# GLU first blocks packed into one PSUM bank, spectral filter rows used at their own pitch, last output in three pieces

## The chip, the cores and the metric

The kernel runs on one core of one Trainium2 chip. Its engines work side by side, each through its own queue in order: TensorE (PE in the profile, its weight loads PEld) for matmuls, VectorE (DVE), ScalarE (ACT), GpSimd (POOL), and SyncE (SP), which here only issues DMAs. The metric is device time in microseconds (us), lower is better. The time before is the median of three runs. The profile is of one more execution, with a time of its own.

## What is computed

The input is 2048 rows of 512 in bf16. A layer norm over each row feeds two branches, whose sum with the input is the output:

```python
xn = _layernorm(x, axis=-1)                       # x: (1, 2048, 512)

# branch A: filter in the frequency domain
X = rfft2(xn, axes=(-2, -1)) * (w_r + 1j * w_i)   # w_r, w_i: (2048, 257)
a = irfft2(X, s=(2048, 512)).astype(bfloat16)

# branch B: gated linear unit
g = xn @ w_gate ; u = xn @ w_up                   # (512, 1792) each
b = (gelu(g) * u) @ w_down                        # (1792, 512)

out = x + a + b
```

## The kernel before

**Tiling.** Row 16p+c of the input is held in partition p, column c: `x_t` and `xn` are [128, 16, 512], and "column c" below means 128 input rows. The 1792 hidden features are 14 weight slices of 128 (`fc`). Four columns form a super-block `sb`, so there are four. For the GLU the normalised rows are needed transposed (`xnT[sb]`): columns 0 to 3 are transposed on TensorE and copied out of PSUM by ScalarE (`pe_transpose`, L445 to L455), columns 4 to 15 by DMA transposes issued by SyncE (L458).

**Order.** Nothing is written in program order. Every piece of work is an operation with an engine, an assumed duration, dependencies, a priority (smaller goes first) and the rings of buffers it takes or frees. `_Plan.run` (L149) plays the list on a model of the engines and emits each operation when the model starts it; on the chip each engine then takes its instructions strictly in that order and waits by semaphores. Loads are modelled in one line of bytes at 0.3e6 bytes per us plus 0.8 us (L195, L196), at most eight in flight. The assumed durations and rates thus decide the order, and nothing else.

**PSUM.** Eight banks: four of tag S (transposes, spectral stages, and the down projection), two of tag G for the gate product, two of tag U for the up product.

**GLU.** `glu(c0, n, fc)` (L492) takes n columns from c0 and one weight slice: four matmuls over 512 inputs into a G bank, four into a U bank (L506), gelu on ScalarE into `ge` (L515), and the product on VectorE into `hT` (L520). The first super-block is done in small units while data arrives: columns 0 and 1 alone with slices 0 and 1, columns 0 and 1 together with slices 2 and 3, columns 2 and 3 with slices 0 to 3, then four columns at a time (L529 to L532). A unit of n columns issues matmuls of 128n wide. Each uses 128n of a bank's 512 columns.

**Start.** x columns 0 to 3 come as four loads, weights in groups 0-1, 2-3, then x 4 to 7, weights 4-6, x 8 to 11, weights 7-9 and 10-13, x 12 to 15 (L334 to L348). `layernorm` takes statistics (L427), adds epsilon (L435), raises to -1/2 on GpSimd (L437) and normalises (L440). TensorE runs ten dummy matmuls from the start, and four small ones after each of the columns 0 and 1 (L406 to L418, `NGAP`).

**Spectral branch.** `fold` (VectorE, L548 to L560, then `bp` matmuls L574), `dstep` (L610, evicted at L615), `cstep` (L630, L638) take the forward transform; `filt` (L644) multiplies by the filter for one of eight groups g; `icstep` (L748) and `idstep` (L796, L802 and the combining at L818 to L824) go back. In `filt`, steps `s3` (L671) and `s4` (L677) multiply 1024 elements by the real and the imaginary filter rows; for g = 0, `s10` (L705 to L708) redoes one partition with seven short instructions as one operation.

**Filter table.** `TW` is [128, 2, 8, 2, 258]: real and imaginary, group, two rows per group, 257 values padded to 258. The weights have 257 values a row, so seven groups of rows are first loaded unpadded into `Ts` (by SyncE at L363, and by indirect DMAs of GpSimd at L365 for the mirrored rows) and then spread by twelve ScalarE copies into `TW` (`spread`, L376, with reversed group order for the mirrored rows); the rows of group 0 come by four more indirect DMAs (L397). GpSimd then mends a few columns (`tables_fix`, L588), which `s3` waits for. `Ts` shares its memory with `Wd`, the down weights, so these are loaded after the copies (L391).

**End.** `down(c)` (L832) sums 14 matmuls with the down weights (L848) and one with the last stage of the inverse transform (L852) in a PSUM bank, adds x on VectorE (L857) and stores (L860). The last column is done in two halves of 256.

Of the kernel before, what the change touches and what calls it, by code (L numbers as in the profile page):

```python
# [10 lines left out]
P = 128  # L11
# [6 lines left out]
S = 2048  # L18
# [110 lines left out]
class _Plan:  # L129
# [19 lines left out]
    def run(self):  # L149
# [11 lines left out]
        while left:  # L161
            nxt, moved = None, False
            for e, ops in waiting.items():
# [30 lines left out]
                if o.nbytes:  # L194
                    wire = max(wire, o.end + 1.0) + o.nbytes / 0.3e6  # L195
                    o.end = wire + 0.8  # L196
                    lanes.append(o.end)
                    lanes = [x for x in lanes if x > now]
# [19 lines left out]
def kernel(  # L218
# [18 lines left out]

    x_v = A_x.rearrange("b (p c) d -> p c (b d)", c=NC)
# [4 lines left out]
    KC = 257  # L243
# [13 lines left out]
    TW = pc.tile([P, 2, NG, 2, 258], BF16, name="TW", tag="TW")  # L257
    TR, TI = TW[:, 0], TW[:, 1]
# [81 lines left out]
    load_x(2, 1)  # L340
    load_x(3, 1)
    load_w(2, 4)
    load_x(4, 4)
    load_w(4, 7)
    load_x(8, 4)
    load_w(7, 10)
# [7 lines left out]
    R7 = 7 * KC  # L354
    d_st = {}

    def load_rows(k, s, h):
        if "Ts" not in tiles:
            tiles["Ts"] = pc.tile([P, 2, 2, R7], BF16, name="Ts", tag="Wd")
        w_in = (A_w_r, A_w_i)[k]  # L360
        rows = w_in.rearrange("(kb t h a g) k -> t h kb a (g k)", kb=NC, t=2, h=2, a=4)
        if s == 0:
            nc.sync.dma_start(out=tiles["Ts"][64 * h:64 * h + 64, k, s], in_=rows[0, h][:, :, KC:8 * KC])  # L363
        else:
            nc.gpsimd.indirect_dma_start(  # L365
                out=tiles["Ts"][:, k, s], out_offset=None, in_=w_in[:, :],
                in_offset=bass.IndirectOffsetOnAxis(ap=idx_t[:, 2:3], axis=0))

    for k in range(2):
        for s in range(2):  # L370
            if s == 0:
                d_st[k, s] = [load(64 * R7 * 2, lambda k=k, s=s, h=h: load_rows(k, s, h)) for h in range(2)]
            else:
                d_st[k, s] = [add("POOL", 1.2, lambda k=k, s=s: load_rows(k, s, 0), (g_idx, XD[12]), 20, lag=5.0)]

    def spread(k, s, g0, g1):  # L376
        T = (TR, TI)[k]
        src = tiles["Ts"][:, k, s].rearrange("p (g k) -> p g k", k=KC)
        src = src[:, g0 - 1:g1 - 1] if s == 0 else src[:, 7 - g1 + 1:7 - g0 + 1][:, ::-1]
        nc.scalar.copy(out=T[:, g0:g1, s, 0:KC], in_=src)  # L380

    for k in range(2):
        for s in range(2):
            for g0, g1 in ((1, 3), (3, 5), (5, 8)):
                d_tw.append(act(0.2 + (g1 - g0) * 0.215, lambda k=k, s=s, g0=g0, g1=g1: spread(k, s, g0, g1),
                                d_st[k, s], 40 + len(d_tw)))

    def load_wd(k):
        if "Wd" not in tiles:
            tiles["Wd"] = pc.tile([P, NFC, D], BF16, name="Wd_sb", tag="Wd")  # L390
        nc.sync.dma_start(out=tiles["Wd"][:, 7 * k:7 * k + 7], in_=wd_v[:, 7 * k:7 * k + 7])  # L391

    d_wd = [load(P * 7 * D * 2, lambda k=k: load_wd(k), d_tw[:12]) for k in range(2)]

    for T, w_in in ((TR, A_w_r), (TI, A_w_i)):
        for s in range(2):
            d_tw.append(add("POOL", 1.2, lambda T=T, w_in=w_in, s=s: nc.gpsimd.indirect_dma_start(  # L397
                out=T[:, 0, s, 0:KC], out_offset=None, in_=w_in[:, :],
                in_offset=bass.IndirectOffsetOnAxis(ap=idx_t[:, s:s + 1], axis=0)), (g_idx, XD[12]), 20, lag=4.0))
# [6 lines left out]
    NWARM, NGAP, GAP = 10, 2, 4  # L406
# [22 lines left out]
    def layernorm(c0, n, due, after=()):  # L429
# [9 lines left out]
        for c in range(c0, c0 + n):  # L439
            XN[c] = dve(0.36, lambda c=c: V.tensor_scalar(  # L440
                out=xn[:, c], in0=x_t[:, c], scalar1=mv[:, c, 0:1], scalar2=rstd[:, c:c + 1],
                op0=ALU.subtract, op1=ALU.mult), (r,), due - 2.5)
        return ag

    def pe_transpose(c, due):  # L445
        b = _Buf("S")

        def mm():
            tp = psum(f"tp.{c}", [P, NE, P], BF16)
            for e in range(NE):  # L450
                nc.tensor.transpose(tp[:, e], xn[:, c, e * P:(e + 1) * P], ident)

        o = pe(0.24, mm, (XN[c], d_ident), due - 2, new=(b,))
        XT[c] = act(0.45, lambda: nc.scalar.copy(out=xnT[c // 4][:, :, c % 4], in_=tiles[f"tp.{c}"][:]),  # L454
                    (o,), due - 30, use=(b,))  # L455

    def dma_transpose(c, due):
        XT[c] = dma(P * D * 2, lambda: nc.sync.dma_start_transpose(out=xnT[c // 4][:, :, c % 4], in_=xn[:, c]),  # L458
                    (XN[c],), due - 30, lag=1.0)

    first = ()
    for c, due in ((0, -28), (1, -25), (2, -22), (3, -19)):
        o = layernorm(c, 1, due, first if c == 1 else ())
        first = o if c == 0 else first
        pe_transpose(c, due)
        if c < NGAP:
            dummies(GAP, due - 1.9, (XN[c],), P)
# [10 lines left out]
    def hslot(sb, fc):  # L478
        if (sb, fc) not in tiles:
            if sb < 3:  # L480
                t = pc.tile([P, NFC, 512], BF16, name=f"hT{sb}", tag=("hT0", "hT1", "xn")[sb])
                tiles.update({(sb, f): t[:, f] for f in range(NFC)})
            else:
                m = min(4, NFC - fc)
                t = pc.tile([P, m, 512], BF16, name=f"hT3{fc}", tag=("xnT0", "xnT1", "xnT2", "hT3")[fc // 4])
                tiles.update({(sb, fc + f): t[:, f] for f in range(m)})
# [3 lines left out]
    done_g = {b: [] for b in range(NSB)}  # L490

    def glu(c0, n, fc, extra=()):  # L492
        sb, o, w = c0 // 4, (c0 % 4) * P, n * P
        gb, ub, eb = _Buf("G"), _Buf("U"), _Buf("ge")
        key = f"{c0}.{n}.{fc}"
        t = now[0]
        dur = 4 * (w / 2400.0 + 0.0024)
        now[0] += 2 * dur + 0.2
# [4 lines left out]
        def mm(nm, W, tag):  # L503
            p = psum(f"{nm}.{key}", [P, D], tag=tag)
            for e in range(NE):
                nc.tensor.matmul(p[:, 0:w], lhsT=W[:, e, fc * P:(fc + 1) * P], rhs=rhs(e),  # L506
                                 start=(e == 0), stop=(e == NE - 1))

        xt = [XT[c] for c in range(c0, c0 + n)]
        g = pe(dur, lambda: mm("g_ps", Wg_sb, "G"), xt + [WD[fc][0]], t, new=(gb,))  # L510
        u = pe(dur, lambda: mm("u_ps", Wu_sb, "U"), xt + [WD[fc][1], g], t, new=(ub,))

        def ge():
            e = work(f"ge.{key}", [P, D], "ge")
            nc.scalar.activation(out=e[:, 0:w], in_=tiles[f"g_ps.{key}"][:, 0:w], func=AF.Gelu_apprx_tanh)  # L515

        a = act(0.1 + w / 1200.0, ge, (g,), t - 40, new=(eb,), use=(gb,))

        def mul():
            V.tensor_tensor(out=hslot(sb, fc)[:, o:o + w], in0=tiles[f"u_ps.{key}"][:, 0:w],  # L520
                            in1=tiles[f"ge.{key}"][:, 0:w], op=ALU.mult)

        h = dve(0.08 + w / 960.0, mul, [u, a] + list(extra), t - 40, use=(ub, eb))
        done_g[sb] += [g, u]
# [378 lines left out]
```

## Time and profile before

| | |
|---|---|
| Time, three runs | 181.13 us median (180.74 to 181.51) |
| Profiled execution | 181.31 us, of which 179.5 from the first to the last instruction |
| TensorE: granted clock | 1.000 |
| DMA | 19.24 MB, mean 107 GB/s, 359 to 409 GB/s in the busiest slices before 23 us |
| GLU matmuls of 512 columns (L506) | 416 of 496; the rest are 256 or 128 wide |
| gelu (L515) at 512, 256, 128 columns | 607, 386, 277 ns |
| product into `hT` (L520) at 512, 256, 128 columns | 686, 410, 285 ns |
| eviction of a transposed column (L454) | 587 ns, 4 times |
| spreading copies (L380) | 12, 738 ns mean, from 29.0 to 46.7 us |
| First `idstep` matmul (L796) | 117.6 us |

The engine shares are averages over stages. Until about 28 us loads run at full rate; from 57 to 108 us the filter groups and the GLU share VectorE; after 122 us TensorE does the down projection with the other engines mostly idle. In a timeline each line gives start, length, engine, line, operation, output <- inputs, and in brackets how long the engine was idle before and what released it. A matmul's listed length contains a modelled pipeline tail, so consecutive rows overlap.

### The profile page before, as it was taken

The numbers are of one execution on the slowest core, as the hardware profiler recorded it, in microseconds if no ns is written. First come the engines' busy times: TensorE is split into PE (matmuls) and PEld (weight loads), VectorE is DVE, ScalarE is ACT, GpSimd is POOL, SyncE is SP. The second block draws the span as 40 slices with busy tenths as digits, with TensorE's granted clock in tenths as the row PEclk, the third lists the DMA queues.
The fourth block names the chain that finished last, engine by engine and source line by source line (L and its number), as shares of the span: only waits on it lengthen the run. The fifth ranks groups of instructions, "written<-read, shape, count | busy, mean of one in ns | idle before, by whom it ended". The sixth has DMA issues, their size and how long they took to land.

```text
span 179.5 us, 2986 instructions
## 1 busy us (share of the span) xinstructions
PE 173.6 (97%) x1057; PEld 91.0 (51%) x1057; DVE 117.9 (66%) x269; ACT 95.6 (53%) x176; POOL 16.4 (9%) x31
## 2 busy tenths in 40 slices
PE   7899999899999999999999999999999999999993
PEld 2596445355554553555555545545445444544462
DVE  1889995999534999989989793436541641632521
ACT  3354225999989849999997945453111211211100
POOL 3404265033200000000000000000000000000000
PEclk9999999999999999999999999999999999999999
DMA  5999999952494002311222022000122231222211
GB/s 146 328 359 347 409 283 160 180 87 58 79 358 151 0 0 55 68 29 29 60 58 64 13 45 45 17 0 0 60 87 64 78 97 58 88 82 68 79 47 50
DMA packets 23182, 19.24 MB, mean 107 GB/s; under 512 B 8256, under 2 KB 21952, under 8 KB 23168
## 3 DMA queue, kind: packets, MB, share of 16 engines
q1 hardware_dynamic: 22176, 17.57, 36.5%
q0 software_dynamic: 320, 1.19, 2.0%
q10 hardware_dynamic: 672, 0.30, 0.6%
q8 instruction: 8, 0.13, 0.3%
q14 instruction: 6, 0.05, 0.1%
HBM read 13.28 MB, written 2.10 MB: 86 GB/s over the span
## 4 chain that ended last, share of the span: by engine, by line
PE 73%; DMA 9%; DVE 7%; SPq 6%; issue 2%; ACT 1%; ACTq 0%; DVEq 0%
PE u_ps L506 18%; PE g_ps L506 17%; DMA Ts<-in_A_w_r_dram 7%; SPq L325 3%; DMA Wu_sb<-in_B_w_up_dram 2%; PE yp L796 2%; PE gp L748 2%; SPq L315 2%; DVE hT L520 2%; PE yp__2064 L848 2%; PE yp__2037 L848 2%; PE yp__2006 L848 2%; PE yp__1921 L848 2%; PE yp__1890 L848 2%; PE yp__1863 L848 2%; PE yp__1832 L848 2%
## 5 line engine op out<-in xcount | busy, mean ns | idle before, releaser
L506 PE MATMUL u_ps<-xnT,Wu_sb 128*128 128x512 bf16 (+2 forms) x248 | 58.2, 358 | 0.6 <-DVE hT L520 0.6
L506 PE MATMUL g_ps<-xnT,Wg_sb 128*128 128x512 bf16 (+2 forms) x248 | 58.2, 358 | 0.5 <-ACT xnT L454 0.5
L520 DVE TENSOR_TENSOR hT<-u_ps,ge 128x512 bf16<-128x512 f32 (+2 forms) x62 | 39.0, 634 | 21.7 <-PE u_ps L506 17.9
L515 ACT ACTIVATE ge<-g_ps 128x512 bf16<-128x512 f32 (+2 forms) x62 | 35.0, 564 | 21.9 <-PE g_ps L506 15.6
L506 PEld LDWEIGHTS <-Wu_sb 128*128 128x128 bf16 x248 | 23.5, 98 | 24.3 <-issue 1.2
L506 PEld LDWEIGHTS <-Wg_sb 128*128 128x128 bf16 x248 | 23.2, 98 | 22.0 <-issue 0.8
L848 PEld LDWEIGHTS <-hT 128*128 128x128 bf16 x238 | 22.7, 98 | 22.0
L802 ACT CAST yf<-yp 128x512 bf16<-128x512 f32 x16 | 9.3, 586 | 38.1 <-PE yp L796 38.1
L638 ACT CAST E<-ep 64x512 bf16<-64x512 f32 x32 | 18.5, 579 | 1.0 <-PE ep L630 0.5
L427 DVE BATCH_NORM_STATS2 st<-x_t 128x6 f32<-128x512 bf16 x16 | 10.7, 675 | 4.3 <-DMA x_t<-in_A_x_dram 4.3
L380 ACT COPY TW<-Ts 128x514 bf16<-128x514 bf16 (+1 forms) x12 | 8.3, 738 | 3.2 <-DMA Ts<-in_A_w_r_dram 3.2
L615 ACT CAST ds<-dp 128x512 bf16<-128x512 f32 x16 | 9.0, 590 | 1.1 <-PE dp L610 1.0
L754 ACT CAST Gs<-gp 128x512 bf16<-128x512 f32 x16 | 8.7, 592 | 1.5 <-PE gp L748 1.5
L437 POOL TENSOR_TENSOR rstd<-ve,half 128x1 f32<-128x1 f32 (+1 forms) x7 | 6.7, 955 | 24.8 <-DVE ve L435 24.8
L578 ACT CAST Bs<-bp 128x512 bf16<-128x512 f32 x16 | 8.7, 633 | 0.0
L411 PE MATMUL warm<-warm 128*128 128x512 bf16 (+1 forms) x18 | 5.5, 469 | 1.3 <-POOL half L404 1.3
L440 DVE TENSOR_SCALAR xn<-x_t,mv,rstd 128x512 bf16<-128x512 bf16 x16 | 6.2, 421 | 0.7 <-POOL rstd L437 0.7
L796 PEld LDWEIGHTS <-Gs 128*128 128x128 bf16 x64 | 4.8, 98 | 3.5
L796 PE MATMUL yp<-CT,Gs 128*128 128x128 bf16 x64 | 6.0, 219 | 0.0
L671 DVE TENSOR_TENSOR m<-X,TW 128x1024 bf16<-128x1024 bf16 x8 | 5.5, 688 | 0.1
L630 PE MATMUL ep<-ds,CT 128*128 128x512 bf16 x16 | 5.6, 379 | 0.0
L677 DVE TENSOR_TENSOR m<-X,TW 128x1024 bf16<-128x1024 bf16 x8 | 5.5, 684 | 0.0
(106 smaller groups left out, 171.1 us busy)
## 6 DMA issues: line engine op xcount, KB each, us to landing
y<-in_A_x_dram SPq DMA_DIRECT2D x16, 128.0 KB, 2.1
F<-F SPq DMA_DIRECT2D x32, 64.0 KB, 2.0
out_dram<-y SPq DMA_DIRECT2D x15, 128.0 KB, 1.7
Wd_sb<-in_B_w_down_dram SPq DMA_DIRECT2D x2, 896.0 KB, 6.3
x_t<-in_A_x_dram SPq DMA_DIRECT2D x3, 512.0 KB, 8.3
Wg_sb<-in_B_w_gate_dram SPq DMA_DIRECT2D x2, 384.0 KB, 7.4
Wu_sb<-in_B_w_up_dram SPq DMA_DIRECT2D x2, 384.0 KB, 8.2
x_t<-in_A_x_dram SPq DMA_DIRECT2D x4, 128.0 KB, 3.4
```

The costliest lines, as they stand in the source:

```text
L380: nc.scalar.copy(out=T[:, g0:g1, s, 0:KC], in_=src)
L427: V.bn_stats(out=st[:], in_=x_t[:, c])
L506: nc.tensor.matmul(p[:, 0:w], lhsT=W[:, e, fc * P:(fc + 1) * P], rhs=rhs(e), start=(e == 0), stop=(e == NE - 1))
L515: nc.scalar.activation(out=e[:, 0:w], in_=tiles[f"g_ps.{key}"][:, 0:w], func=AF.Gelu_apprx_tanh)
L520: V.tensor_tensor(out=hslot(sb, fc)[:, o:o + w], in0=tiles[f"u_ps.{key}"][:, 0:w], in1=tiles[f"ge.{key}"][:, 0:w], op=ALU.mult)
L578: nc.scalar.copy(out=o, in_=tiles[f"bp.{cg}.{q}"][:].rearrange("p c (r g a) -> p (c r) g a", r=2, a=4))
L615: nc.scalar.copy(out=ds[:].rearrange("p (s k t) -> p s k t", s=2, t=2), in_=tiles[f"dp.{G}"][:].rearrange("p s t k -> p s k t"))
L638: nc.scalar.copy(out=tiles[f"E.{g}"][64 * h:64 * h + 64, r], in_=tiles[f"ep.{g}.{h}"][64 * r:64 * r + 64])
L754: nc.scalar.copy(out=o, in_=tiles[f"gp.{g}.{h}"][:].rearrange("p q (n a) -> p (q n) a", a=4))
L796: nc.tensor.matmul(yp[:, q], lhsT=tiles["G"][:, q, c], rhs=IQ[q], start=(q == 0), stop=(q == 3), skip_group_check=True)
L802: nc.scalar.copy(out=tiles[f"yf.{c // 2}"][:, c % 2], in_=tiles[f"yp.{c}"][:])
L848: nc.tensor.matmul(y[:, s], lhsT=tiles[sb, f][:, cl * P:(cl + 1) * P], rhs=tiles["Wd"][:, f, s], start=(f == 0), stop=False)
```

## The change

Five groups of edits.

1. **First blocks.** `glu(c0, n, f0, nf)` now takes nf weight slices for n columns into one bank, each at its own 128n columns of it, with one gelu and one product over nf x 128n columns. The gate and up matmuls are issued two slices at a time. The first super-block becomes six packed units and then slices 6 to 13 for four columns. Loads are regrouped: x columns 2 and 3 in one, weights in 0-1, 2-3, 4-5 ahead of x 4 to 7, then 6-9 and 10-13. The planner's load model becomes 0.34e6 bytes per us plus 1.0 us.
2. **Start.** Column 0 is normalised, transposed and evicted in two halves, the second eviction by VectorE. Columns 2 and 3 share one `layernorm`, whose statistics wait for column 0's evictions. One set of small dummies instead of two.
3. **Filter table.** `TW` becomes [128, 2, 2, 8 x 257] without padding; the loads and indirect DMAs write it directly, `Ts` and the copies are gone, and `s3`, `s4`, `s10` and `tables_fix` read and write it at pitch 257, the mirrored rows in descending group order. The down weights have their own tile and load after the last forward fold.
4. **Filter order.** `s10` is planned as seven operations; buffers `ds` and `E` are claimed by the matmul ahead of the eviction, and the four `E` evictions are no longer chained to the first.
5. **End.** The down projection uses the G and U banks in turn, and the last column is done in pieces of 256, 128 and 128.

The core of the diff:

```diff
-                    wire = max(wire, o.end + 1.0) + o.nbytes / 0.3e6
-                    o.end = wire + 0.8
+                    wire = max(wire, o.end + 1.0) + o.nbytes / 0.34e6
+                    o.end = wire + 1.0
...
-    TW = pc.tile([P, 2, NG, 2, 258], BF16, name="TW", tag="TW")
-    TR, TI = TW[:, 0], TW[:, 1]
+    TW = pc.tile([P, 2, 2, NG * KC], BF16, name="TW", tag="TW")
...
-    load_x(2, 1)
-    load_x(3, 1)
+    load_x(2, 2)
     load_w(2, 4)
+    load_w(4, 6)
     load_x(4, 4)
-    load_w(4, 7)
+    load_w(6, 10)
     load_x(8, 4)
-    load_w(7, 10)
     load_w(10, 14)
...
+    def rows_at(s, g):
+        return (7 - g if s else g) * KC
+
+    def pair(k, g, p=P):
+        a = TW[0:p, k, 0, rows_at(0, g):rows_at(0, g) + 256]
+        step = NG * KC + rows_at(1, g) - rows_at(0, g)
+        return bass.AP(a.tensor, a.offset, [a.ap[0], [step, 2], [1, 256]])
+
+    def load_rows(k, h):
+        rows = (A_w_r, A_w_i)[k].rearrange("(kb t h a g) k -> t h kb a (g k)", kb=NC, t=2, h=2, a=4)
+        nc.sync.dma_start(out=TW[64 * h:64 * h + 64, k, 0, KC:], in_=rows[0, h][:, :, KC:8 * KC])
+
+    def gather(k, s, c, a, n):
+        w_in = (A_w_r, A_w_i)[k]
+        nc.gpsimd.indirect_dma_start(
+            out=TW[:, k, s, a:a + n], out_offset=None, in_=w_in[:, :],
+            in_offset=bass.IndirectOffsetOnAxis(ap=idx_t[:, c:c + 1], axis=0))
...
-    def spread(k, s, g0, g1):
-        T = (TR, TI)[k]
-        src = tiles["Ts"][:, k, s].rearrange("p (g k) -> p g k", k=KC)
-        src = src[:, g0 - 1:g1 - 1] if s == 0 else src[:, 7 - g1 + 1:7 - g0 + 1][:, ::-1]
-        nc.scalar.copy(out=T[:, g0:g1, s, 0:KC], in_=src)
...
-    NWARM, NGAP, GAP = 10, 2, 4
+    NWARM, NGAP, GAP = 10, 1, 4
...
+            for h in range(halves):
+                d = slice(h * D // halves, (h + 1) * D // halves)
+                XN[c].append(dve(0.04 + 0.29 / halves, lambda c=c, d=d: V.tensor_scalar(
+                    out=xn[:, c, d], in0=x_t[:, c, d], scalar1=mv[:, c, 0:1], scalar2=rstd[:, c:c + 1],
+                    op0=ALU.subtract, op1=ALU.mult), (r,), due - 2.5))
...
+            def ev(es=es, eng=(nc.scalar.copy, V.tensor_copy)[h]):
+                eng(out=xnT[c // 4][:, es[0]:es[-1] + 1, c % 4], in_=tiles[f"tp.{c}"][:, es[0]:es[-1] + 1])
...
+    first = layernorm(0, 1, -28, (), 2)
+    layernorm(1, 1, -25, first)
+    for c in range(4):
+        if c == 2:
+            layernorm(2, 2, -22, XT[0])
+        pe_transpose(c, -28 + 3 * c)
...
+            for f in range(a, b):
+                for e in range(NE):
+                    nc.tensor.matmul(tiles[f"{nm}.{key}"][:, f * w:f * w + w], lhsT=W[:, e, (f0 + f) * P:(f0 + f + 1) * P],
+                                     rhs=rhs(e), start=(f + e == 0), stop=(f == nf - 1 and e == NE - 1),
+                                     skip_group_check=nf > 1)
...
-    units = [(0, 1, 0), (0, 1, 1), (1, 1, 0), (1, 1, 1), (0, 2, 2), (0, 2, 3)]
-    units += [(2, 2, fc) for fc in range(4)] + [(0, 4, fc) for fc in range(4, NFC)]
+    FIRST = [(0, 1, 0, 4), (1, 1, 0, 4), (0, 2, 4, 2), (2, 2, 0, 2), (2, 2, 2, 2), (2, 2, 4, 2)]
+    for c, n, f, nf in FIRST + [(0, 4, f, 1) for f in range(6, NFC)]:
+        glu(c, n, f, nf)
...
-        tr = TR[:, g, :, 0:256].unsqueeze(1).to_broadcast([P, 2, 2, 256])
-        ti = TI[:, g, :, 0:256].unsqueeze(1).to_broadcast([P, 2, 2, 256])
+        tr, ti = (pair(k, g).unsqueeze(1).to_broadcast([P, 2, 2, 256]) for k in range(2))
...
-            last = dve(2.2, s10, [last], t, new=(ab,), use=(eb, fb))
+            for n in range(7):
+                last = dve(0.34, lambda n=n: s10(n), [last], t, new=(ab,) if n == 0 else (), use=(ab, eb, fb))
...
-        parts = 2 if c == NC - 1 else 1
-        for k in range(parts):
-            pb = _Buf("S")
-            s = slice(k * D // parts, (k + 1) * D // parts)
+        cuts = (0, 256, 384, 512) if c == NC - 1 else (0, 512)
+        for k in range(len(cuts) - 1):
+            tag = "GU"[(c + k) % 2]
+            pb = _Buf(tag)
+            s = slice(cuts[k], cuts[k + 1])
+            parts = D // (cuts[k + 1] - cuts[k])
```

## The prediction

> **What bounds the kernel now.** I read the page's busy shares first, then TensorE's rows in order of time, then who was late at each of its gaps. Parts 1 and 2 of the page:
>
> ```profile
> PE 173.6 (97%) x1057; PEld 91.0 (51%) x1057; DVE 117.9 (66%) x269; ACT 95.6 (53%) x176; POOL 16.4 (9%) x31
> PE   7899999899999999999999999999999999999993
> DVE  1889995999534999989989793436541641632521
> PEclk9999999999999999999999999999999999999999
> ```
>
> TensorE is busy throughout at full granted clock, so the span is its work plus its gaps. A "busy" row ends with a modelled tail, so I measure gaps by starts: four 128x512 matmuls are issued every 0.863 us (0.2158 each), four 128x128 every 0.222 (0.0556 each), four 128x256 every 0.437 (0.1092 each). TensorE's timeline (start, length, engine, line; in brackets what it waited for):
>
> ```profile
> 7.27 0.38 PE L506 MATMUL g_ps<-xnT,Wg_sb 128*128 128x128 bf16 x4 [0.25 <-ACT xnT L454]
> 8.16 0.39 PE L411 MATMUL warm<-warm 128*128 128x128 bf16 x4
> 8.38 0.39 PE L506 MATMUL u_ps<-xnT,Wu_sb 128*128 128x128 bf16 x4
> 9.00 0.38 PE L506 MATMUL g_ps<-xnT,Wg_sb 128*128 128x128 bf16 x4 [0.23 <-ACT xnT L454]
> ...
> 32.01 1.03 PE L506 MATMUL g_ps<-xnT,Wg_sb 128*128 128x512 bf16 x4
> 33.31 1.02 PE L506 MATMUL u_ps<-xnT,Wu_sb 128*128 128x512 bf16 x4 [0.27 <-DVE hT L520]
> 35.03 0.39 PE L574 MATMUL bp<-RF_t,xf 128*128 128x128 bf16 x4
> 35.77 0.84 PE L574 MATMUL bp<-RF_t,xf 128*128 128x128 bf16 x12 [0.35 <-DVE xf L560]
> ...
> 68.08 1.03 PE L506 MATMUL g_ps<-xnT,Wg_sb 128*128 128x512 bf16 x4
> 69.48 1.02 PE L506 MATMUL u_ps<-xnT,Wu_sb 128*128 128x512 bf16 x4 [0.37 <-DVE hT L520]
> ```
>
> Real work begins at 7.27. Lost after it: 9.00-8.38-0.22 = 0.40, the dummies 0.22, 33.31-32.01-0.86 = 0.44, 35.77-35.03-0.22 = 0.52, 69.48-68.08-0.86 = 0.54. Together 2.12 us: that, the lead-in and the tail are all that can be won.
>
> Who is late at 33 and 35 us is in ScalarE's timeline:
>
> ```profile
> 25.27 0.60 ACT L515 ACTIVATE ge<-g_ps 128x512 bf16<-128x512 f32 x1 [1.13 <-PE g_ps L506]
> 29.02 0.62 ACT L380 COPY TW<-Ts 128x514 bf16<-128x514 bf16 x1 [3.15 <-DMA Ts<-in_A_w_r_dram]
> 29.54 0.59 ACT L515 ACTIVATE ge<-g_ps 128x512 bf16<-128x512 f32 x1
> ```
>
> The first spreading copy holds ScalarE's queue for 3.15 us until its filter rows land; the gelu behind it is late, VectorE then idles 2.24 us for that gelu (its row at 30.17), and the folds and hT behind that reach TensorE late. At 69 us it is VectorE: the one-partition fix-up of filter group 0 (L705 to L708) runs from 65.81 to 68.4 in one block, and the hT that frees TensorE's bank starts at 68.73.
>
> **The change, part by part.**
>
> *Lead-in.* Column 0 is normalised, transposed and evicted in two halves, one evicted by ScalarE and one by VectorE. Now: xn 5.52, transposes 5.99, copy 6.63 to 7.21, matmul 7.27. A half normalisation is not in the trace: above the 0.15 of the 128x1 row at L435, below the 0.41 of the whole; I take 0.3. Second half: 5.52+0.3+0.3 = 6.1, two transposes and their latency 0.3, eviction 0.41 (the 128x256 row of L520), hop 0.05: 6.9 to 7.0. Gain 0.3, bounds 0 and 0.5.
>
> *First blocks.* The second set of dummies goes (0.22), and 9.00's wait for column 1 (0.40) should go, since columns 2 and 3 may now take statistics only after column 0 is out, so column 1's normalisation no longer stands behind two 0.65 us statistics rows. Added: 160 matmuls of sb 0 become 192. Before, 32x0.0556+48x0.1092+80x0.2158 = 24.28; after, 64x0.0556+64x0.1092+64x0.2158 = 24.36: +0.08. New wait: weight slices 2 and 3 are wanted 16x0.0556 = 0.89 after the first matmul, gate at 7.9 and up at 8.3; they were issued at 3.16 and 3.64 and 256 KB loads landed after 4.5 and 5.0: 7.7 and 8.6. That is a wait of 0.3; bounds 0 (the merged x load frees one issue) and 1.0. Behind it in TensorE's queue stands column 1's block, and everything after. Slices 4 and 5 are wanted near 11.1; they take the bytes' place of x columns 4 to 7, which landed at 10.47: in time by 0.6. Part: -0.62+0.08+0.3 = -0.24.
>
> *Filter rows in place.* ScalarE loses the twelve copies (8.3 us busy) and the 3.15 us hold. Gaps of 0.44+0.52 = 0.96 should close. What is late next: columns 4 to 7 now arrive behind 512 KB more weights (about 1.4 us at the 354 GB/s of 10 to 15 us) and VectorE is busy 12.78 of 13.50 us from 15 to 28.5, so their normalisation and SyncE's transposes move back; the last of those four transposes was issued near 28.7 and lands after a median 3.5, about 32.2, against a first block-1 matmul that moves from 34.17 to about 33.2. Margin 1.0 less that delay: I give back 0.3; bounds 0 and 0.96. Part: -0.66. POOL's six gathers and four row loads move the same bytes; the column fix ended at 48.8 and its reader starts at 59.00, ten microseconds of cover. The down weights get their own tile, load at 47.5 as before, and are wanted at 121.86. Zero for both.
>
> *The multiplies at pitch 257.* They were 0.684 to 0.688 us for 1024 elements, sixteen of them. Rows at the new pitch start on odd elements in one of each pair. The forms by group that price this (busy, mean ns):
>
> ```profile
> L671 DVE TENSOR_TENSOR m<-X,TW 128x1024 bf16<-128x1024 bf16 x8 | 5.5, 688 | 0.1
> L681 DVE TENSOR_TENSOR Y<-m,m 128x512 bf16<-128x512 bf16 x8 | 3.3, 418 | 0.1
> L548 DVE TENSOR_TENSOR A<-xn 128x1024 bf16<-128x1024 bf16 x4 | 2.7, 678 | 0.0
> ```
>
> and, from VectorE's timeline, two rows with an fp32 source:
>
> ```profile
> 173.36 0.69 DVE L857 TENSOR_TENSOR y<-yp__2090,y 128x512 bf16<-128x512 f32 x1 [2.55 <-PE yp__2090 L852]
> 175.00 0.42 DVE L857 TENSOR_TENSOR y<-yp__2110,y 128x256 bf16<-128x256 f32 x1 [0.94 <-PE yp__2110 L852]
> ```
>
> bf16 costs (688-418)/512 = 0.53 ns an element, the fp32 source (0.69-0.42)/256 = 1.05. If the odd start drops a multiply to the latter, it costs 1024x0.52 = 0.53 us more; sixteen are 8.5, and four 512-wide ones of the fix-up 1.1: 9.6 us. The other end is zero. The nearest row is L548, whose second operand begins at element 511, byte 1022, no multiple of four, and still runs at 678 ns; but it reads backwards, so its pairs lie on whole words. I take zero and keep 9.6.
>
> [...]
>
> *Fix-up in seven pieces.* hT can come between; the 0.54 at 69.48 shrinks. I take 0.4, bounds 0 and 0.54. Buffers E and ds are claimed at the matmul instead of the eviction, which reorders only.
>
> *Last output in three.* Matmuls 15x2x0.0556 = 1.668 for 15x0.1092 = 1.638: +0.03. Last eviction 0.285 (128-wide row of L520) for 0.425: -0.14. Half the store: 128 KB landed in 1.7, 64 KB in 1.5, so 0 to -0.2; I take -0.04. Part: -0.15. Evictions come 0.83 apart, longer than a store's issue (0.34).
>
> **Sum.** -0.30-0.24-0.66-0.40-0.15 = -1.75. The profiled execution took 181.31 (span 179.50 and 1.81 around it): 179.56. It lies 0.18 above the runs' median of 181.13, so 179.4 for the median. All bounds for the good: 178.5; the lesser losses: 180.3.
>
> **Rivals.** *The waits come back elsewhere.* The order of every engine is fixed in advance by an assumed 340 KB/us for loads where it was 300; the 2.08 MB up to x columns 4 to 7 had landed at 10.47, 0.21 MB/us counted from 0.73. Orders that believe loads early park an in-order engine behind one that is late, as L380 did. If the 0.24, 0.66 and 0.40 are all lost to this, 180.7. For it: VectorE's full stretch to 28 us. Against: TensorE was not stopped between 10.33 and 32.87. *Slower: odd rows halve the multiply.* From 57 to 108 us VectorE idles 1.01+3.33 = 4.34 us, which it would absorb; that decides from 4.34/16 = 0.27 extra for each, a multiply above 0.95 us. At the full price 9.6-4.3 = 5.3 reaches TensorE through its two up banks, which hT frees: 184.7; nothing absorbed, 189. For it: an odd forward start is not shown. Against: L548.
>
> **Chances and range.** Forecast 0.61, waits come back 0.20, slower 0.19. 0.5% (about what this measurement can tell) is 0.9 us: faster is below 180.2, slower above 182.0. Faster: nearly all of the first, a fifth of the second, 0.63; same 0.16; slower 0.21. The likeliest case alone spans 178.5 to 180.3. With the second case and the milder part of the third, 178.4 to 182.4.
>
> **What would show it.** L671 and L677 near 0.69 us (right) or near 1.2 (the slower rival). No ScalarE wait between 25 and 29 us and no TensorE gaps near 33 and 35; none above 0.2 near 68. First gate matmul near 6.95. A gap before the second up step at 8.3 names the weight loads. Wrong altogether if TensorE shows new gaps of over 1 us behind hT between 57 and 110, or waits for xnT when block 1 starts.

## The result, and the profile after

The changed kernel took 187.61 us (median of 4 runs, 186.14 to 191.22); the kernel before, on the same chip, 180.94 (4 runs, 180.71 to 181.51). The ratio is 1.034, 95% interval 1.026 to 1.042. The forecast of 179.4 and its range to 182.4 were both missed, on the other side of no change. Medians here are of all runs, while the ratios and their intervals leave out slow runs, for these kernels those over 1.5% above the fastest of the same kernel. The profiled execution took 186.14 us, with a span of 184.3.

Parts 1 and 2 of the page of the changed kernel:

```profile
PE 174.2 (94%) x1100; PEld 92.8 (50%) x1100; DVE 118.1 (64%) x265; ACT 87.5 (47%) x158; POOL 16.1 (9%) x32
PE   7799999269999999999999999999999999999994
DVE  2759999707953789598999998426434434434432
PEclk9999999969999999999999999999999999999999
```

Two slices of 4.6 us show a hole ("2", then "6"), and the granted clock has a dip in the second. TensorE's timeline there:

```profile
32.43 1.03 PE L498 MATMUL u_ps<-xnT,Wu_sb 128*128 128x512 bf16 x4
38.40 1.86 PE L498 MATMUL g_ps<-xnT,Wg_sb 128*128 128x512 bf16 x4 [4.94 <-DMA xnT<-xn]
40.06 1.78 PE L498 MATMUL u_ps<-xnT,Wu_sb 128*128 128x512 bf16 x4
41.67 1.03 PE L498 MATMUL g_ps<-xnT,Wg_sb 128*128 128x512 bf16 x4
```

38.40 is the first matmul of block 1. By starts it is 38.40-32.43-0.86 = 5.11 us late, and the bracket names the transposes of columns 4 to 7. The next eight matmuls need 41.67-38.40 = 3.27 us where eight take 8x0.2158 = 1.73: 1.54 more. The windows of the same stretch say why; behind the five engines' busy times stand the granted clock, the DMA share and GB/s:

```profile
33.00:38.00 5.00, 0.46 (x3) 0.00 (x0) 2.91 (x6) 0.23 (x1) 0.00 (x0) 1.00 1.39 189
38.00:40.00 2.00, 1.60 (x4) 0.58 (x5) 0.00 (x0) 0.00 (x0) 1.23 (x6) 0.54 0.98 197
40.00:42.00 2.00, 2.00 (x7) 0.78 (x6) 0.06 (x1) 0.60 (x1) 0.00 (x0) 0.61 0.00 0
42.00:44.00 2.00, 2.00 (x23) 1.38 (x21) 1.97 (x5) 1.26 (x3) 0.54 (x1) 1.00 0.00 0
```

After the idle stretch the clock was granted at about half (0.54 and 0.61 in these windows). Wait and slow clock are 5.11+1.54 = 6.65 us. The profiled executions differ by 186.14-181.31 = 4.83, so everything else gained 6.65-4.83 = 1.82. Of that, 0.47 is the first load, which landed earlier in this execution (first statistics row at 3.18 for 3.65), and 1.35 is left for the change. The forecast without its give-back was 2.05.

The chain that ended last, in order of time, has the culprit as one piece (start, us, what):

```profile
28.00 10.26 DMA xnT<-xn
38.40 1.86 PE g_ps L498 x4
```

That is the fourth transpose of block 1: issued at 28.00, landed 10.26 us later. Before, the same four were issued at 20.38, 21.78, 24.86 and 27.62 and landed at 30.7, 31.5, 32.2 and 33.3. What stood ahead of them in SyncE's queue had landed at about the same time in both kernels (row loads by 30.0 before, an output prefetch by 30.3 after), and yet the four land from 33.1 to 38.3 now. Beside them, on GpSimd's timeline of the changed kernel, stand its software gathers of filter rows (L366):

```profile
19.08 1.01 POOL L416 TENSOR_TENSOR rstd<-ve,half 128x4 f32<-128x4 f32 x1 [9.64 <-DVE ve L414]
20.27 1.10 POOL L366 DMA_INDIRECT TW<-in_A_w_r_dram,idx_t  x1 [0.18 <-issue]
...
24.19 1.36 POOL L366 DMA_INDIRECT TW<-in_A_w_i_dram,idx_t  x1 [0.31 <-issue]
25.62 1.27 POOL L416 TENSOR_TENSOR rstd<-ve,half 128x4 f32<-128x4 f32 x1
27.09 0.99 POOL L366 DMA_INDIRECT TW<-in_A_w_i_dram,idx_t  x1 [0.19 <-issue]
```

Before, the reciprocal of columns 4 to 7 (`rstd`) stood at 15.47, and the two large gathers left at 16.66 and 18.06 and had landed by 26.9. Now x columns 4 to 7 land at 12.6 instead of 10.47 and VectorE reaches them late. `rstd` goes at 19.08, and the large gathers, which stand behind it in GpSimd's queue, at 20.27 and 24.19. The large imaginary one landed at 35.3 and the two small ones at 36.0 and 38.1; transposes two to four at 35.3, 36.0 and 38.3. They end in pairs.

### The profile page after: what moved, and what is told of

Its sections match the earlier page's. It is cut to its first block, busy times and chain, and to the rows that moved or that the text cites. A ratio compares the mean times of both kernels' runs of the same rounds, so it can differ in the third digit from the quotient of the medians.

```text
span 184.3 us, 3039 instructions
## 1 busy us (share of the span) xinstructions
PE 174.2 (94%) x1100; PEld 92.8 (50%) x1100; DVE 118.1 (64%) x265; ACT 87.5 (47%) x158; POOL 16.1 (9%) x32
## 4 chain that ended last, share of the span: by engine, by line
PE 73%; DVE 10%; DMA 9%; ACT 4%; issue 2%; SPq 1%; DVEq 0%
PE u_ps L498 18%; PE g_ps L498 18%; DMA xnT<-xn 6%; DMA Wu_sb<-in_B_w_up_dram 3%; DVE hT L523 3%; DVE st L406 3%; ACT E L648 2%; PE yp L814 2%; PE gp L763 2%; PE yp__2076 L868 2%; PE yp__2050 L868 2%; PE yp__2023 L868 2%; PE yp__1992 L868 2%; PE yp__1965 L868 2%; PE yp__1876 L868 2%
## 5 line engine op out<-in xcount | busy, mean ns | idle before, releaser
L498 PE MATMUL g_ps<-xnT,Wg_sb 128*128 128x512 bf16 (+2 forms) x264 | 58.9, 350 | 5.2 <-DMA xnT<-xn 4.9
L523 DVE TENSOR_TENSOR hT<-u_ps,ge 128x512 bf16<-128x512 f32 x56 | 38.3, 684 | 24.5 <-PE u_ps L498 21.8
L515 ACT ACTIVATE ge<-g_ps 128x512 bf16<-128x512 f32 x56 | 33.5, 598 | 37.5 <-PE g_ps L498 32.8
L498 PEld LDWEIGHTS <-Wg_sb 128*128 128x128 bf16 x264 | 24.2, 98 | 26.8 <-issue 6.9
L498 PEld LDWEIGHTS <-Wu_sb 128*128 128x128 bf16 x264 | 24.5, 99 | 23.3 <-issue 1.1
L416 POOL TENSOR_TENSOR rstd<-ve,half 128x4 f32<-128x4 f32 (+2 forms) x6 | 5.5, 924 | 19.2 <-DVE ve L414 19.1
L422 DVE TENSOR_SCALAR xn<-x_t,mv,rstd 128x512 bf16<-128x512 bf16 (+1 forms) x17 | 6.0, 399 | 0.0
L620 PEld LDWEIGHTS <-Bs 128*128 128x128 bf16 x64 | 4.4, 98 | 2.4
L763 PEld LDWEIGHTS <-F 128*128 128x128 bf16 x64 | 4.3, 98 | 2.1 <-issue 0.2
```

The lines of the kernel that those rows point to most:

```text
L498: nc.tensor.matmul(tiles[f"{nm}.{key}"][:, f * w:f * w + w], lhsT=W[:, e, (f0 + f) * P:(f0 + f + 1) * P], rhs=rhs(e), start=(f + e == 0), ...
L515: nc.scalar.activation(out=e[:, 0:nf * w], in_=tiles[f"g_ps.{key}"][:, 0:nf * w], func=AF.Gelu_apprx_tanh)
L523: V.tensor_tensor(out=out, in0=tiles[f"u_ps.{key}"][:, 0:nf * w].rearrange("p (f w) -> p f w", w=w) if nf > 1 else tiles[f"u_ps.{key}"][:, ...
L763: nc.tensor.matmul(gp[:, q], lhsT=F[:, h, q % 2, q // 2::2], rhs=cc("M" if 2 * g + h else "M0"), start=(q == 0), stop=(q == 3), skip_group ...
```

## Experiments

Three theories came out of that. **G**: the gathers share the DMA engines with block 1's transposes and hold them up. **X**: the late x columns 4 to 7 alone do it. **Q**: it is the output prefetches that now stand ahead of the transposes in SyncE's queue. Each kernel is measured against the kernel before on the same chip.

**e1_x_first: x columns 4 to 7 ahead of weight slices 4 and 5 again.**

```diff
-    load_w(4, 6)
     load_x(4, 4)
+    load_w(4, 6)
```

> The changed kernel with x columns 4 to 7 loaded ahead of weight slices 4 and 5 again. Theory G (the large gathers of GpSimd are on the DMA engines together with block 1's four transposes): the rstd in front of the gathers comes about 1.5 us earlier, the gathers with it, so the last transpose lands at 35 to 37 us instead of 38.3; time 183 to 186. Theory X (it is the late arrival of x columns 4 to 7 alone that makes block 1 late): the first transpose is issued near 21 us, the last lands near 33, no wait over 1 us; time 179 to 180.5. Theory Q (two prefetches of x stand ahead of the transposes in SyncE's queue): here the prefetches come after them, so also 33 to 35 and 180 to 182.

Measured: 186.56 us, ratio 1.020 (1.016 to 1.025), and a wait of 5.14 us for xnT. Early columns brought the reciprocal to 16.53 and the first transposes to 19.98 and 21.37, and the wait stayed. So X alone falls; G's range of 183 to 186 was missed by 0.6 as well. In the same order of queues the prefetches stand behind the transposes, which speaks against Q.

**e2_gathers_after: all six gathers wait for block 1's transposes,** through a small GpSimd operation that reads what the transposes wrote.

```diff
+    o_gate = add("POOL", 0.2, lambda: nc.gpsimd.tensor_scalar(out=gate[0:1, :],
+        in0=xnT[1][0:1, 0, :, 0], ...), [o for c in range(4, 8) for o in XT[c]], 19, lag=0.05)
...
-                            (g_idx, XD[12]), 20, lag=5.0))
+                            (g_idx, XD[12], o_gate), 20, lag=5.0))
```

> The changed kernel with one small GpSimd instruction that reads block 1's transposed rows put ahead of the six gathers, so that these start only when the four transposes have landed. Theory G: the transposes land 1 us apart from about 31 us, the last at 33 to 34.5, TensorE's wait at block 1 is under 1.5 us, the clock stays full; time 179 to 181. Theories X and Q: transposes are issued at 23 to 28 us as before behind the same queue, the last still lands at 37 to 38; time 185.5 to 188.

Measured: 181.03 us (10 runs, 180.58 to 181.80), ratio 1.0005 (0.998 to 1.003); no wait ahead of block 1. Its view of DMA issues from 22 to 29 us (queue, kind, count, median us to landing), and the held operation on GpSimd:

```profile
xnT<-xn SPq DMA_TRANSPOSE x4, 3.3
```

```profile
30.75 0.22 POOL L462 TENSOR_SCALAR gate<-xnT 1x4 bf16<-1x4 bf16 x1 [4.22 <-DMA xnT<-xn]
31.50 1.28 POOL L366 DMA_INDIRECT TW<-in_A_w_r_dram,idx_t  x1 [0.54 <-issue]
```

With no gather in flight the transposes, issued between 23.78 and 28.07, take a median of 3.3 us (4.25, 3.26 and 2.49 for the three whose landing is in the trace), where the changed kernel's took 10.1. G holds. The kernel does not win what the rest of the change should bring: 0.84+0.22+0.13+0.25 = 1.44 us are lost by starts between 40 and 48 us, the longest of it as a wait for hT (0.68). Why VectorE is late there was not followed further.

**e3_prefetch_after: the output prefetches wait for the transposes.**

```diff
-        l = dma(P * D * 2, ld, (), t - 12, new=(yb,))
+        l = dma(P * D * 2, ld, [o for j in range(4, NC) for o in XT[j]], t - 12, new=(yb,))
```

> The changed kernel with the x prefetches of the down stage made to wait for all transposes. Theory Q: 0.25 MB leave the queue ahead of the transposes and two issues with them, the last lands 3 us earlier or more; time 181 to 183. Theory G: 0.7 us of transfer at most, the last lands at 37 to 38; time 185 to 187.5. Theory X: the same as G.

Measured: 188.07 us, ratio 1.032 (1.025 to 1.040), wait 7.23 us. Q falls; the time is also 0.6 above G's range.

**b2_filter_only: the kernel before with only the filter rows used in place** (table, loads, gathers, views and their own tile for the down weights from the change; all else as before).

```diff
-    TW = pc.tile([P, 2, NG, 2, 258], BF16, name="TW", tag="TW")
+    TW = pc.tile([P, 2, 2, NG * KC], BF16, name="TW", tag="TW")
...
-        tr = TR[:, g, :, 0:256].unsqueeze(1).to_broadcast([P, 2, 2, 256])
+        tr, ti = (pair(k, g).unsqueeze(1).to_broadcast([P, 2, 2, 256]) for k in range(2))
```

> The kernel before with the filter table alone changed (unpadded in place, no spreading copies, own tile for the down weights); loads, first blocks, end and planner rates as before. Theory G: the order of GpSimd puts the large imaginary gather behind the second group's rstd (about 24 us), beside the transposes, so the last lands at 35 us or later and the kernel is slower than before: 182 to 186. Theory X: x columns 4 to 7 are early, so block 1 is in time and the gaps of 0.44 and 0.52 near 33 and 35 us close: 179.8 to 180.6.

Measured: 180.11 us (10 runs, 179.76 to 181.67), ratio 0.997 (0.994 to 0.9995), no gap of TensorE above 0.1 us after 9.4 us. The number G gave was wrong, and the one X gave was met, although e1 had spoken against X. GpSimd's timeline shows which gather is late here:

```profile
23.97 1.42 POOL L417 TENSOR_TENSOR rstd<-ve,half 128x4 f32<-128x4 f32 x1 [4.71 <-DVE ve L415]
25.58 1.00 POOL L367 DMA_INDIRECT TW<-in_A_w_r_dram,idx_t  x1 [0.19 <-issue]
26.88 0.96 POOL L367 DMA_INDIRECT TW<-in_A_w_i_dram,idx_t  x1 [0.30 <-issue]
```

A large gather issued at 26.88, after the first transposes had left at 20.65 and 22.05, did no harm. In the changed kernel, e1 and e3 the second large one came between 21 and 25 us. So G had to be narrowed: **H**, the jam needs a second large gather that is already queued when block 1's transposes begin to move. Its rivals: **L**, the lateness of the change's columns and transposes is what is needed, and **R**, the number of gathers in a row.

**b3_gathers_in_row: b2_filter_only with its six gathers in a row** behind the first reciprocal (large imaginary at 20.77).

```diff
-                            (g_idx, XD[12]), 20, lag=5.0))
+                            (g_idx, XD[12]), -40, lag=5.0))
```

> The kernel of b2_filter_only (180.11 us, no stall) with one thing moved: all six gathers are issued in a row behind the reciprocal of columns 4 to 7, the large imaginary one about 20.8 us after the start instead of 26.9; loads, transposes and tables are as in b2. Theory H: what stalls block 1 is a second large gather that is already queued when block 1's transposes begin to move (about 26 us): their packets then alternate and each waits for the other. H expects the stall in this kernel too, though no load comes later: TensorE waits 2 to 6 us for xnT ahead of block 1, 183 to 188 us. Rival L (late columns 4 to 7 and the later transposes of the change are what is needed, with gathers or without): no such wait, 180 to 181 us.

Measured: 180.54 us, but 10 runs from 179.63 to 184.49. The profiled one, at 181.7, has a wait of 1.39 us for xnT; its first transpose, issued at 20.00, landed at 34.1. Fault added, wait added, but smaller than expected and not in every run. H's number of 183 to 188 fails, and the median is the one L gave.

**g2_big_imag_held and g1_imag_held: the changed kernel with some gathers held** by the same small operation: in g2 the large imaginary one, in g1 all three imaginary ones.

```diff
     for k in range(2):
         for c, s, a, n in (...):
+            if k == 1:                 # g2: if k == 1 and c == 2
+                continue
             d_tw.append(add("POOL", 1.2, ..., (g_idx, XD[12]), 20, lag=5.0))
...
+            d_tw.append(add("POOL", 1.2, ..., (g_idx, XD[12], o_gate), 20, lag=5.0))
```

> The changed kernel with one gather held back, the large imaginary one, until block 1's four transposes have landed; the other five are issued in a row as before, about 20 to 27 us. H expects no wait for xnT ahead of block 1 (under 1 us), 179 to 182 us. Rival R (what counts is the number of gathers queued in a row, four or more, whatever their size): the wait of 3 to 6 us stays, 184 to 188 us. L: the wait stays as well.

> The changed kernel with the three imaginary gathers, one large and two small, held back until block 1's four transposes have landed; the three real ones stay at 20 to 23 us. H and R both expect no wait for xnT ahead of block 1, 178.5 to 181 us; L expects the wait to stay, 184 to 188 us. Against e2_gathers_after, where all six were held, the gathers and the table's fix-up end some us earlier.

Measured: g2 181.38 us (10 runs), ratio 0.998 (0.995 to 1.002), wait 1.42. g1 **179.78** us (9 runs, 179.27 to 181.19), ratio 0.993 (0.989 to 0.997), no wait. L falls: in g1 the columns are as late (`rstd` at 19.28) and the transposes leave as late (23.42 to 27.85). Between H and R g2 doesn't decide: its wait is longer than H said and shorter than R said. The two small imaginary gathers, all that g2 leaves in place and g1 holds, still cost something (1.42 us of wait, none in g1), far less than with the large one (4.94). TensorE in g1 at the start of block 1:

```profile
32.76 1.03 PE L511 MATMUL u_ps<-xnT,Wu_sb 128*128 128x512 bf16 x4
33.62 1.03 PE L511 MATMUL g_ps<-xnT,Wg_sb 128*128 128x512 bf16 x4
34.49 1.03 PE L511 MATMUL u_ps<-xnT,Wu_sb 128*128 128x512 bf16 x4
```

**e4_old_rates: the changed kernel with the planner's two old constants.**

```diff
-                    wire = max(wire, o.end + 1.0) + o.nbytes / 0.34e6
-                    o.end = wire + 1.0
+                    wire = max(wire, o.end + 1.0) + o.nbytes / 0.3e6
+                    o.end = wire + 0.8
```

> The changed kernel with the planner's two constants for loads as before the change (300 KB/us and 0.8 us). The gathers are then ordered differently on GpSimd: the reciprocal of block 2's columns comes between the real three and the imaginary three, so the large imaginary gather is issued some 2 us later or more, behind that reciprocal; the output prefetches also come behind block 1's transposes. H expects no wait or a short one (0 to 2 us), 179 to 183 us: the two constants are then the part of the change that brings the stall. If the wait of 4 to 6 us stays, the order of these two is not what decides, and the late loads are: 185 to 188 us.

Measured: 183.02 us (4 runs, 181.21 to 184.73). In the profiled execution the second reciprocal stands ahead of the imaginary gathers, the large one leaves at 28.55, after all four transposes (21.76 to 26.23), and block 1 doesn't wait. The median lies just above what H expected, and the two runs near 184.6 have no profile: that these constants are all of it isn't shown.

**h1_plain_load and h2_hw_queue: an ordinary load of as many bytes in place of the large imaginary gather,** from GpSimd's queue (h1) and from ScalarE's (h2). Both bring other rows.

```diff
+        if k == 1 and c == 2:
+            rows = w_in.rearrange("(p r) k -> p (r k)", p=P)[:, 0:n]
+            nc.gpsimd.dma_start(out=TW[:, k, s, a:a + n], in_=rows)   # h2: nc.scalar.dma_start
+            return
```

> The changed kernel with its large imaginary gather replaced by an ordinary load of as many bytes, from the same GpSimd queue and at the same place in it (it brings other rows, so the imaginary table's second half is not the reference's). If it is the gather, its rows picked one by one, that blocks the transposes, the wait for xnT ahead of block 1 falls to about what g2_big_imag_held showed, 1 to 2 us, and the time to 180 to 182 us. If any 460 KB in flight beside the transposes do it, the wait stays at 4 to 6 us and the time at 185 to 188.

> The changed kernel with its large imaginary gather replaced by an ordinary load of as many bytes that ScalarE issues, about 20 to 24 us after the start, so in a hardware queue and not in GpSimd's software queue (it brings other rows, so the imaginary table's second half is not the reference's). If what blocks the transposes is large packets of the software queue, the wait for xnT ahead of block 1 falls to about that of g2_big_imag_held (0 to 1.6 us), 179 to 182 us. If any 460 KB in flight beside them do it, the wait is 3 to 6 us, 183 to 188 us. A wait of the second kind in one execution and none in another would say that neither alone decides.

Measured: h1 184.19 us with runs from 180.57 to 188.59, wait 1.70 in the profiled one. h2 182.85 us (181.85 to 185.80), wait 2.31 in the profiled one, the longest of the four; its load left at 25.58, later than meant, and held ScalarE's queue, which cost TensorE 1.28 us at 26.7. Neither settles whether it must be a gather or a software queue. The two times fit neither expectation; h1's wait is the one expected if it is the gather. Nor do the waits show that the load did it: the other five gathers were still there, and g2, with neither load nor large imaginary gather there, waited 1.42 us. The two runs of h1 near 187 and 189 us have no profile.

**b1_x_late: the kernel before, two loads exchanged.**

```diff
-    load_x(4, 4)
     load_w(4, 7)
+    load_x(4, 4)
```

> The kernel before with one thing changed: the loads of weight slices 4 to 6 stand ahead of x columns 4 to 7, so those land some 2 us later; the two large gathers then leave GpSimd back to back near 19 and 21 us instead of 16.7 and 18.1, and block 1's transposes leave later too. If a large gather still in flight when those transposes start is what stalls block 1, this order of loads alone brings the stall to the kernel before: a wait for xnT of 1 to 6 us ahead of block 1, 182.5 to 187 us. If the gathers land in time or lateness does nothing, 180.5 to 182 us and no wait over 0.5 us there.

Measured: 184.42 us (4 runs: 181.79, 182.72, 186.12, 188.34); the two lower ones alone give a ratio of 1.007 (1.001 to 1.012). The profiled execution, 188.34, on TensorE and on GpSimd:

```profile
33.91 1.03 PE L506 MATMUL u_ps<-xnT,Wu_sb 128*128 128x512 bf16 x4
41.11 1.87 PE L506 MATMUL g_ps<-xnT,Wg_sb 128*128 128x512 bf16 x4 [6.17 <-DMA xnT<-xn]
```

```profile
19.29 1.02 POOL L437 TENSOR_TENSOR rstd<-ve,half 128x4 f32<-128x4 f32 x1 [9.85 <-DVE ve L435]
20.49 1.09 POOL L365 DMA_INDIRECT Ts<-in_A_w_r_dram,idx_t  x1 [0.18 <-issue]
21.89 0.95 POOL L365 DMA_INDIRECT Ts<-in_A_w_i_dram,idx_t  x1 [0.30 <-issue]
```

This is the shortest road to the fault: none of the change's parts but an order of two loads like its own. Late columns move the reciprocal from 15.47 to 19.29, the two large gathers move with it, and block 1 waits 6.17 us. Two of the small gathers, at 23.14 and 24.40, and an output prefetch at 20.28 moved forward with them. The runs at 181.8 and 182.7 can have had little of it.

**f1_fix_whole: g1_imag_held with the one-partition fix-up in one piece again.**

```diff
-            for n in range(7):
-                last = dve(0.34, lambda n=n: s10(n), [last], t, new=(ab,) if n == 0 else (), use=(ab, eb, fb))
+            last = dve(2.2, lambda: [s10(n) for n in range(7)], [last], t, new=(ab,), use=(ab, eb, fb))
```

> The kernel of g1_imag_held (179.78 us) with the one-partition fix-up of filter group 0 in one piece again, all else as in the change. The prediction's step (the fix-up alone makes the 0.54 us gap near 69 us, splitting it wins 0.4) expects a gap of 0.5 to 0.6 us at that up step in place of 0.28, 180.0 to 180.3 us against 179.8. The rival, from b2_filter_only, which had the fix-up whole and no gap there: the gap came with VectorE being late from the spreading copies on, and splitting wins nothing; 0 to 0.3 us of gap, 179.4 to 179.9.

Measured: **179.34** us (6 runs, 179.07 to 180.43), ratio 0.992 (0.989 to 0.994): the lowest median of the fourteen kernels, though its interval overlaps g1's. That is 0.06 below the rival's range. The gap of 0.28 us in g1 is gone. It did not stand at the up step, as the expectation has it, but between matmuls of the inverse transform, three units of which come in a row there (76.61-75.66-12x0.0556 = 0.28):

```profile
75.66 1.11 PE L776 MATMUL gp<-CT,F 128*128 128x128 bf16 x12
76.61 1.03 PE L511 MATMUL u_ps<-xnT,Wu_sb 128*128 128x512 bf16 x4
```

At the up step neither kernel has a gap. On VectorE the fix-up ends at 64.5, and the next hT follows at once:

```profile
64.00 0.41 DVE L736 TENSOR_TENSOR F<-u 1x512 bf16<-1x512 bf16 x1
64.45 0.16 DVE L729 TENSOR_TENSOR F<-E,t 1x4 bf16<-1x4 bf16 x1
64.53 1.29 DVE L536 TENSOR_TENSOR hT<-u_ps,ge 128x512 bf16<-128x512 f32 x2
```

**All runs side by side.** A transpose of one column is 512 DMA packets of 256 bytes, so four are 2048. How many packets under 512 bytes started between 28 and 33 us is a measure of how the transposes moved; the DMA view counts them. Here of the changed kernel, of f1_fix_whole and of b1_x_late, each with the software queue's line:

```profile
DMA packets 794, 0.41 MB, mean 82 GB/s; under 512 B 731, under 2 KB 766, under 8 KB 793
q0 software_dynamic: 35, 0.19, 32.3%
```

```profile
DMA packets 2406, 0.70 MB, mean 141 GB/s; under 512 B 2260, under 2 KB 2405, under 8 KB 2405
q0 software_dynamic: 1, 0.00, 0.0%
```

```profile
DMA packets 181, 0.15 MB, mean 30 GB/s; under 512 B 156, under 2 KB 164, under 8 KB 181
q0 software_dynamic: 24, 0.11, 10.0%
```

| kernel | small packets, 28 to 33 us | wait for xnT ahead of block 1, us | median us |
|---|---|---|---|
| before | 2101 | 0 | 180.94 |
| e2, all six held | 2216 | 0 | 181.03 |
| g1, imaginary three held | 2266 | 0 | 179.78 |
| f1, g1 with whole fix-up | 2260 | 0 | 179.34 |
| h1, plain load | 2107 | 1.70 | 184.19 |
| g2, large imaginary held | 1844 | 1.42 | 181.38 |
| b2, filter rows alone | 1750 | 0 | 180.11 |
| e4, old constants | 1733 | 0 | 183.02 |
| b3, six in a row | 983 | 1.39 | 180.54 |
| e1, x first | 758 | 5.14 | 186.56 |
| after | 731 | 4.94 | 187.61 |
| e3, prefetches after | 717 | 7.23 | 188.07 |
| h2, plain load from ScalarE | 368 | 2.31 | 182.85 |
| b1, two loads exchanged | 156 | 6.17 | 184.42 |

The count follows the wait only roughly: h1 has 2107 and a wait, b2 and e4 have 1750 and 1733 and none. In b1_x_late both queues together moved 0.15 MB in 5 us, 30 GB/s, where the kernel before moved 186. The transfers do not share a full pipe; they stand. Packets of a large gather, at a median of 0.28 to 0.37 us each, took up to 1.96 us in the changed kernel, 5.66 in e1 and 7.48 in b1, and at most 0.90 before. Slow packets alone are not the jam: in e2, without a wait, they took up to 1.35. With the imaginary gathers or all six held (e2, g1, f1: 25 runs) no run was above 181.80. What stays open: whether a row gather is needed or any large transfer does it, why the two kinds of transfer hold each other up, and what decides, in kernels at the edge (b3, b1, h1), which runs jam. b2_filter_only had both kinds in flight and both moved.

## Why the prediction was wrong, point by point

**The step that failed** is the give-back of the filter part: "the last of those four transposes was issued near 28.7 and lands after a median 3.5, about 32.2 ... Margin 1.0 less that delay: I give back 0.3; bounds 0 and 0.96". The issue time was near enough (27.62 before, 28.00 after). The duration was not: 3.5 us was the median over twelve transposes, eight of which belong to later blocks, and the four of block 1 had taken 10.3, 9.7, 7.4 and 5.7 us in that very trace. The last landed at 33.3, not 32.2, so the margin to 34.17 was 0.85 before anything moved, and nothing of it was left at 33.29, when the changed kernel wants them. The upper bound of 0.96 was no bound: it was the gain being lost, not the wait that could arise. The wait was 5.11 us, and 1.54 of slow clock came on top, which the sum had no term for.

**The second mis-sized term** is its neighbour: "POOL's six gathers and four row loads move the same bytes ... Zero for both." The cover named was that of their own reader, ten microseconds, and it held. Whom they meet on the way was not asked. They stand behind the reciprocal of columns 4 to 7 on GpSimd, so the late x loads moved them too, by 3.6 us and more, onto the transposes. e2 and g1 take them away from there and the wait is gone; b1 puts them there in the kernel before and it comes.

**Lead-in, 0.30:** seen in some executions only. From VectorE's first statistics row to the first gate matmul: 7.27-3.65 = 3.62 before, 6.45-3.18 = 3.27 after, 0.35 less. In b2, b3 and b1, which have the old lead-in, it was 3.40 to 3.41; in f1, e1 and h1, which have the new one, 3.47 to 3.53. So it is between -0.1 and +0.35, by execution.

**First blocks, 0.24:** not seen. From the first gate matmul to the point where eight whole slices remain: before 19.03-7.27 = 11.76, after 18.59-6.45 = 12.14, in e2 11.76, in g1 11.44. The wait for weight slices 2 and 3 came where it was put, 0.47 at 8.82 for the 0.3 assumed. Unforeseen were 0.22 in the first block, whose second half of columns waits for VectorE's eviction, and 0.14 at 7.91. Between -0.3 and +0.4 us, by execution.

**Filter rows, 0.96 of gaps:** right. In b2_filter_only, where nothing else changed, none of the gaps near 33 and 35 us is left, and the one at 69 is gone too.

**Multiplies, zero:** right, and the rival of the halved rate is out. The groups after:

```profile
L679 DVE TENSOR_TENSOR m<-X,TW 128x1024 bf16<-128x1024 bf16 x8 | 5.5, 692 | 0.2
L685 DVE TENSOR_TENSOR m<-X,TW 128x1024 bf16<-128x1024 bf16 x8 | 5.5, 684 | 0.0
```

692 and 684 ns stand where 688 and 684 stood: bf16 rows that start on odd elements, one in each pair, added at most 4 ns. That whole words matter, as the argument on L548 has it, was the author's assumption; no run shows it.

**Fix-up, 0.40:** not seen. The gap at the up step is gone with the fix-up split (after, e2, g1) and with the fix-up whole (b2, f1), so the split is not what closed it. Split, a gap of 0.28 us stands at the inverse transform; whole, none. From the first gate matmul to the end of the span g1 and f1 take 170.5 and 170.6 us, the same. In b2, where the fix-up is as before, VectorE reaches it at 62.98 for 65.81; that the ScalarE hold made it late before is likely, not shown.

**Last output, 0.15:** about right. From the start of the down phase to the last matmul 54.72 us for 54.64; from there to the end of the span 184.3-181.42 = 2.88 for 179.5-176.33 = 3.17: 0.21 less.

**The sum.** With the gathers out of the way (g1) the change is worth 1.50 us of median (179.78 against 181.28 of its own before), where the sum, give-back included, said 1.75. Right in kind was the rival of returning waits; its price, 180.7, had the same flaw as the bound. The signs named for "wrong altogether" held the one that came: TensorE waits for xnT when block 1 starts.

## What to carry to other kernels

Take a transfer's duration from the instances in question, not from the median of its group, and bound a wait by what can stand behind it, not by the gain that it would undo. When a load moves, follow every queue whose instructions wait for it, down to the DMAs that other engines issue behind that wait, and ask whom these meet in flight. Large gathers and on-the-way transposes were best kept apart in time: holding three gathers back until four transposes had landed turned a loss of 3.4% into a gain of 0.7%, for one operation of 0.23 us on GpSimd, which in the changed kernel is busy for 9% of the span.

## What the runs showed of the hardware that was not expected

- **Transposes and large gathers in flight together can both be slow.** Four DMA transposes took a median of 3.3 us with no gather beside them (e2) and 10.1 (changed kernel) and 13.6 (b1) with gathers, while all DMA together moved 82 and 30 GB/s between 28 and 33 us. Packets of the large gathers took up to 1.96 us in the changed kernel and 7.48 in b1, and at most 0.90 before. No run here shows the mechanism.
- **A wait can cost more than its length.** After 5 us of idleness TensorE's clock lost 2x0.46+2x0.39 = 1.70 us between 38 and 42 us, as much as 3.4 us at half; 0.50 was granted from 38.4 to 41.5. In the executions of e1 and e3, after waits of 5.1 and 7.2 us, half clock was granted for 6.8 us in both (means of 0.982), some of it already in the wait. It also came after a shorter wait: in h2 one of 2.31 us was followed, 1.2 us after the matmuls went on, by 0.50 from 38.7 to 42.0. After waits of 1.39 to 1.70 us (b3, g2, h1) the clock stayed full (means of 0.998, 1.000 and 1.000). The profiled execution of e4, without a wait ahead of block 1, had a mean of 0.990.
- **The first load varies by a microsecond.** x column 0 had landed by 3.18 to 4.20 us in the fourteen profiled executions (start of the first statistics row), and the first gate matmul moves with it, 6.45 to 7.50. That is as large as most terms of the sum, so such terms are read from differences within a trace and not from the span.
